# Pair 0's C scaled from PSUM, and four moves in the queues of a fused scan and feed-forward kernel

## The chip, the cores and the metric

The kernel runs on one core of one Trainium2 chip. The metric is the device time of one execution in microseconds (us), the median of several runs. A core has TensorE (PE; its weight loads are PEld), VectorE (DVE), ScalarE (ACT), GpSimd (POOL) and SyncE (SP), each with a queue of its own that is worked off in order. SP, ACT and POOL also issue DMA transfers. PE writes only to PSUM, eight banks of 512 fp32 columns on 128 partitions; the other tiles lie in SBUF.

## What is computed

The first half is a chunked scan over a sequence of 768 for 4 batches and 8 heads, with a state of 16 x 32 per head; its output is fed to a bilinear layer over 3072 tokens (256 to 1536 to 256).

```python
cum = np.cumsum(log_a_chunk, axis=-1)
L = np.exp(cum[..., :, None] - cum[..., None, :]) * causal
M = np.einsum('bhin,bhjn->bhij', Cc, Bc) * L
y = np.einsum('bhij,bhjd->bhid', M, xc) + np.einsum('bhin,bhnd->bhid', Cc, state) * np.exp(cum)[..., None]
state = decay_full * state + sum_j(B_j x_j * decay_from_j)
...
out = ((y @ w_a) * (y @ w_b)) @ w_out
```

## The kernel before, in words

The sequence is cut into 6 blocks of 128 positions, and two batches form a pair, so there are 12 pairs; pair p is block p // 2. Everything is done pair by pair, in an order that is written out by hand for pairs 0 to 2 and by a loop over p = 3 to 11 after that (lines 579 to 778). Each engine gets its instructions in the order of the code.

The decay is split into two factors: fC multiplies C and fB, its reciprocal, multiplies B. Running products of `a` come from `scan` on DVE (L204, one block each), their reciprocal at mid-block from `over_mid` (L207), and `sel_over_mid` (L210, tile selr) spreads it. `factors_mm` (L223) turns them by small fp32 matmuls into a PSUM bank, fps, of 32 columns per block. ACT copies fps to fC; `fb` (L569) makes fB of fC on DVE. For block 0 DVE makes fB straight from fps (L585).

For each pair, `scale_bc` (L261, L253) multiplies B and C by their factors (tiles bm and cm) and `scale_x` (L245, L247) turns x to fp16. For pairs 0 to 3, `transposes` (L288) turns bm and cm on PE; ACT copies the turned B (bt, L299, masked by the constant ch) and DVE the turned C (ct, L300). From pair 4 on, POOL writes bm and cm into the tile planes (L253, L271) and `turn` (L310) has a transposing DMA on SP's queue turn them. `scores` (L322) are 32 small matmuls into the tile SC; `mask` (L356 on DVE, or L353 on ACT with L354 on POOL, through the tile tmp) makes them causal; `pv`, `pv_u` and `outputs` (L365, L399, L427) form the pair's output, and `ds_mm` (L382) the state's increment. ACT copies the output to X2T (L418, L443; for pair 0 L453 and L455; for pair 2 half on ACT, half on DVE, L414 and L415). `state_sums` (L468, L470, tile U) updates the state on DVE and `state_spread` (L486, L493, tiles spair and gU) prepares it on POOL for the pair of the next block; `state` calls both.

The feed-forward layer is cut into 6 units per pair. `unit` has PE make two products of 4 matmuls each, aps (with Wa) and bps (with Wb), at L506; ACT copies aps to asb (L520), and DVE multiplies bps by asb into hk (L527). `out_mm` (L540) multiplies hk by Wo, 12 matmuls for each batch of the pair; ACT copies this down result to osb (L555, `out_store`) and SP stores it (L557). The PSUM tiles aps, bps, ops, fps, py, tb, tc and gps share four banks.

Pair p's B, C and x are loaded in two halves each (`load1`, L126), into one of three buffers. Loads of the start go over the queues of SP, ACT and POOL; POOL also loads the weights (L142, L147). From pair 3 on all loads, all turning transfers and nearly all stores go over SP. The constants ch (from ph, 5 KB) and c32 are loaded at L178 and L165. `warmup` (L197) issues matmuls of zeros whose results nobody reads, so that PE is busy in the start; the text calls them dummies.

Of the kernel before, what the change touches and what calls it, by code (L numbers as in the profile page):

```python
# [9 lines left out]
f32 = mybir.dt.float32  # L10
# [12 lines left out]
def kernel(  # L23
# [13 lines left out]
    nc = tc.nc  # L37
# [4 lines left out]
    NBLK = S // Q  # L42
# [74 lines left out]
    def tiles(p):  # L117
        Bn = inp.tile([128, H, 2, N], f32, name="bn", tag="bn")
        Cn = inp.tile([128, H, 2, N], f32, name="cn", tag="cn")
        Xn = inp.tile([128, H, 2, D], f32, name="xn", tag="xn")  # L120
        pair_in[p] = (Bn, Cn, Xn)

    def load1(eng, p, which, bt, i0=0, n=64):
        blk, bp = divmod(p, NBP)
        src = (B, C, x)[which][2 * bp + bt, :, blk * Q + 2 * i0 : blk * Q + 2 * i0 + 2 * n, :]
        return eng.dma_start(  # L126
            pair_in[p][which][64 * bt + i0 : 64 * bt + i0 + n].rearrange("i h r n -> i h (r n)"),
            src.rearrange("h (i r) n -> i h (r n)", r=2),
        )
# [2 lines left out]
        tiles(p)  # L132
        return [load1(eng or nc.sync, p, w, bt) for w in range(3) for bt in range(2)]

    def load_parts(p):
        tiles(p)
        return lambda w: [load1(nc.sync, p, w, bt) for bt in range(2)]

    def load_w(half):
        c = slice(half * KC, (half + 1) * KC)  # L140
        return [
# [14 lines left out]
    load1(nc.sync, 0, 0, 0)  # L156
    load1(nc.scalar, 0, 1, 1)
    load1(nc.sync, 0, 1, 0, 0, 32)
    load1(nc.scalar, 0, 1, 0, 32, 32)
    nc.scalar.preload_act_table_set("natural_log_exp_and_others")  # L160
    load1(nc.scalar, 0, 2, 1)
    load1(nc.sync, 0, 2, 0)
    load1(nc.scalar, 1, 1, 1)
    load1(nc.sync, 1, 0, 0)
    nc.sync.dma_start(c32, p32_t.ap())  # L165
    nc.vector.memset(warm.bitcast(u32), 0)  # L166
    nc.vector.memset(zero, 0.0)
# [7 lines left out]
        pattern=[[-H, 2], [-2 * H, NBP], [-1, H]],  # L175
        channel_multiplier=1,
    )
    nc.gpsimd.dma_start(ch, ph_t.ap())  # L178
    nc.gpsimd.memset(ident, 1.0)
    nc.gpsimd.affine_select(  # L180
        out=ident, in_=ident, compare_op=ALU.is_equal, fill=0.0, base=0, pattern=[[-1, 128]], channel_multiplier=1
# [20 lines left out]
    def scan(lo, hi):  # L202
        for k in range(lo, hi):
            nc.vector.tensor_tensor_scan(Pr[:, k], a_sb[:, k], zero, 1.0, ALU.mult, ALU.add)  # L204
# [9 lines left out]
            op=ALU.mult,  # L214
        )

    def factors_mm(lo, hi):
        fps = psf.tile([128, 512], f32, name="fps", tag="ff")
        F = fps[:, 0 : (hi - lo) * 2 * NBP * H].rearrange("p (k r c) -> p k r c", k=hi - lo, r=2)
        for k in range(lo, hi):  # L220
            for r in range(2):
                for bt in range(2):
                    nc.tensor.matmul(  # L223
                        F[64 * bt : 64 * bt + 64, k - lo, r],
                        Pr[:, k].rearrange("p (i r) -> p r i", r=2)[:, r],
                        selr[:, k, bt],
                        start=True,
                        stop=True,
                        skip_group_check=True,
                        tile_position=(0, 64 * bt),  # L230
                    )
        return F.rearrange("p k r c -> p (k r c)")

    def flat(f, lo, hi):
        return f[:, lo:hi].rearrange("p k r b h -> p (k r b h)")
# [10 lines left out]
        else:  # L246
            eng.tensor_scalar(xo, xi, XS, None, ALU.mult)  # L247

    def scale_bc(p, which, eng):
        blk, bp = divmod(p, NBP)  # L250
        name, f = (("bm", fB), ("cm", fC))[which]
        if p >= P0 and which:
            eng.tensor_tensor(  # L253
                out=planes[p % 2][:, 4:6].rearrange("p r (h n) -> p r h n", n=N),
                in0=pair_in[p][which].rearrange("p h r n -> p r h n"),
                in1=f[:, blk, :, bp].unsqueeze(3).broadcast_to((128, 2, H, N)),
                op=ALU.mult,
            )
            return
        m_ = mid.tile([128, 2, H, N], f16, name=name, tag=name)  # L260
        eng.tensor_tensor(  # L261
            out=m_,
            in0=pair_in[p][which].rearrange("p h r n -> p r h n"),
            in1=f[:, blk, :, bp].unsqueeze(3).broadcast_to((128, 2, H, N)),
            op=ALU.mult,
        )
        st.setdefault(p, {})[name] = m_
        if p >= P0:
            dst = planes[p % 2][:, 0:4].rearrange("p (r e) (m f n) -> p r e m f n", e=2, f=2, n=N)
            for e in range(2):  # L270
                eng.tensor_copy(dst[:, :, e, :, e], m_.rearrange("p r (m f) n -> p r m f n", f=2)[:, :, :, e])  # L271
# [6 lines left out]
    def transposes(p, ps=None, between=None, apart=False):  # L278
        s = st[p]
        if ps is None:  # L280
            ps = [SC[0], SC[1]] if apart else None
            on_dve = apart
        else:
            on_dve = True
        TB, TC = (TT[:, 0:256], TT[:, 256:512]) if ps is None else [t_.bitcast(f16)[:, 0:256] for t_ in ps]
        for T_, src in ((TB, s["bm"]), (TC, s["cm"])):
            for r in range(2):
                nc.tensor.transpose(  # L288
                    T_[:, r * 128 : (r + 1) * 128], src[:, r].rearrange("p h n -> p (h n)"), ident
                )  # L290
            if between:
                between()
                between = None
        BT = mid.tile([128, 2, 2, 2, 64], f16, name="bt", tag="bt")
        CT = mid.tile([128, 2, Q], f16, name="ct", tag="ct")
        b_ = []
        for e in range(2):
            o_ = BT[:, e].rearrange("p r t i -> p (r t i)")
            b_.append(nc.scalar.activation(out=o_, in_=TB, func=AF.Copy, scale=par[:, e : e + 1]))  # L299
        c_ = (nc.vector.tensor_copy if on_dve else nc.scalar.copy)(  # L300
            CT.rearrange("p t (i r) -> p r (t i)", r=2), TC.rearrange("p (r c) -> p r c", r=2)
        )
        if apart:
            for i_ in b_:
                tc.declare_no_dep(c_.ins, i_.ins.name, reason="reads of two banks")
        s["BT"], s["CT"] = BT, CT
# [276 lines left out]
    sel_over_mid(0, 1, nc.vector)  # L583
    v = factors_mm(0, 1)
    nc.vector.reciprocal(flat(fB, 0, 1), v)  # L585
    nc.scalar.copy(flat(fC, 0, 1), v)
    warmup(2, SC[3])
    warmup(1, SC[3], 128)
    scale_bc(0, 0, nc.vector)
    scale_bc(0, 1, nc.vector)  # L590
    scan(1, 3)
    tb, tcp = bank("tb"), bank("tc")
    transposes(0, [tb, tcp], lambda: warmup(1, SC[3]))
    over_mid(1, 3)
    sel_over_mid(1, 3, nc.vector)
    warmup(1, SC[3])
    warmup(2, SC[3], 128)
    scores(0)
# [2 lines left out]
    mask(product0(0, 1))  # L601
    mask(product0(1, 1), by_pool=True)
    mask(product0(1, 0))
    v = factors_mm(1, 3)
    nc.scalar.copy(flat(fC, 1, 3), v)  # L605
    warmup(2, tcp)
    scale_bc(1, 1, nc.vector)
    scale_bc(1, 0, nc.gpsimd)
    py = [bank("py0"), bank("py1")]
    pv_u(0, 0, py, True)  # L610
# [21 lines left out]
    scale_x(1, nc.scalar)  # L632
    for m in range(2):
        mask(product(1, m))
    over_mid(3, NBLK)
    sel_over_mid(3, NBLK, nc.vector)
    mask(product(1, 2))
    bps = [unit_mm(0, k2, Wb) for k2 in range(3)]
    for bt in range(2):
# [13 lines left out]
    tc.add_manual_dep(x2[0].ins, w1[1].ins.name, AFTER, reason="weights ahead of pair 2's x")  # L653
    for k2 in range(3):
        times(0, k2, bps[k2], asb[k2])
    v = factors_mm(3, NBLK)
    pv(1, DS=(0, SC[:2]))
    ds_mm(0, 64, SC[:2])
    nc.scalar.copy(flat(fC, 3, NBLK), v)
    fb(1)  # L660
    scale_bc(2, 0, nc.gpsimd)
    scale_bc(2, 1, nc.gpsimd)
# [24 lines left out]
    h()  # L687
    scale_x(2, nc.scalar)
    scale(3)
    o = [bank("ops"), bank("ops")]  # L690
    out_mm(0, 0, o[0], range(6))
    out_mm(0, 1, o[1], range(6))
    out_mm(0, 0, o[0], range(6, NK))
    pull(2)
    pv(2, split=True)
    out_mm(0, 1, o[1], range(6, NK))
    h = unit(2, 0)
    transposes(3, apart=True)
    load(4)
    for bt in range(2):  # L700
        out_store(0, bt, o[bt])
    state(2)
    fb(2)
    h()
    h = unit(2, 1)
# [1 line left out]
    for p in range(3, NP):  # L707
        scores(p)
        ri = p >= P0
        if p + 1 < NP:  # L710
            scale(p + 1)
        if p + 2 < NP:
            loads = load_parts(p + 2)
            loads(0)
            if ri:
                loads(1)
        if p + 1 < NP:
            turn(p + 1)
        if p + 2 < NP:
            if not ri:  # L720
                loads(1)
            loads(2)
        if p == 3:
            mask(product(p, 0))
            h()
            for m in range(1, 4):
                mask(product(p, m))
            out_half(1, 0)
            out_half(1, 1)
            go((2, 2))  # L730
        else:
            h = unit(p - 1, 0)
            mask(product(p, 0), ri=ri)
            h()
            mask(product(p, 1), ri=ri)
            mask(product(p, 2), ri=ri)
            h = unit(p - 1, 1)
            h()
            mask(product(p, 3), ri=ri)
            go((p - 1, 2))  # L740
            out_half(p - 2, 0)
            go((p - 1, 3))
        pull(p)
        outputs(p) if ri else pv(p)
        state(p)
        if p == 3:
            go((2, 3))
        else:
            out_half(p - 2, 1)
        if p % 2 == 0 and p // 2 + 1 < NBLK:  # L750
            fb(p // 2 + 1)
        go((p - 1, 4), (p - 1, 5))
# [56 lines left out]
```

## Time and profile before

| what | value |
|---|---|
| median of 3 runs | 128.59 us (128.12 to 130.98) |
| the profiled execution | 130.67 us, its span 129.0 us |
| PE busy | 122.5 us (95%), 1963 matmuls |
| DVE, ACT, POOL busy | 89.0, 72.6, 56.9 us |
| DMA | 13.79 MB in 45877 packets, 40896 of them under 512 B |
| turning transfer (L310) | 8, 2.9 us from issue to landing (median) |
| hk (L527) | 72, 686 ns each |
| asb (L520) | 72, 587 ns each |

The span is the time from the first instruction to the last in the profiled execution; its execution's own time has some 1.7 us around that. A busy PE is not PE at its peak, since the ends of its pipelined matmuls are modelled. In timelines the first column is the start and the second the duration in us, rows that are alike are merged (x8), and brackets hold the idle time ahead of the first and what ended it. ACTq, SPq and POOLq are the queues' own work, mostly the issue of transfers.

### The profile page before, as it was taken

To read this page: it belongs to the slowest core of one execution; us is meant where nothing else is said; L and a number is where in the kernel's file an instruction comes from. 1 tells how busy PE (TensorE), PEld (TensorE's weight loads), DVE (VectorE), ACT (ScalarE), POOL (GpSimd) and SP (SyncE) were. 2 spreads that over 40 slices of the span, in tenths; PEclk is the share of its full clock that TensorE was granted. 3 is DMA by queue.
4 is the path that set the end of the run, shared out by engine and by line. 5 is a ranking of instruction groups with operands and counts; after the bars stand their busy time and mean duration, and the time that the engine had idled before them with its cause. 6 is when DMAs were issued, how large, how long until landed. Compare 5 with 4: busy or idle time off the path is not lost.

```text
span 129.0 us, 4787 instructions
## 1 busy us (share of the span) xinstructions
PE 122.5 (95%) x1963; PEld 102.2 (79%) x1963; DVE 89.0 (69%) x167; ACT 72.6 (56%) x145; POOL 56.9 (44%) x100
## 2 busy tenths in 40 slices
PE   6999979999899998999999999999999999999990
PEld 2454768988588986988988988988898889899980
DVE  1586695985677985884976967967939939834450
ACT  0464646781646547547556576476575485585530
POOL 6979596759662545605607508309128000000000
PEclk9999999999999999999999999999999999999999
DMA  3999999975526569972793473644732210110112
GB/s 67 188 119 232 145 192 175 186 147 86 140 42 119 149 111 116 173 163 74 119 125 92 69 171 80 118 126 88 133 91 76 50 64 5 41 41 5 41 41 81
DMA packets 45877, 13.79 MB, mean 107 GB/s; under 512 B 40896, under 2 KB 45664, under 8 KB 45856
## 3 DMA queue, kind: packets, MB, share of 16 engines
q1 hardware_dynamic: 41376, 10.05, 39.2%
q0 software_dynamic: 1952, 3.02, 14.4%
q10 hardware_dynamic: 2528, 0.43, 2.0%
q8 instruction: 15, 0.25, 0.9%
q14 instruction: 6, 0.05, 0.2%
HBM read 11.13 MB, written 3.15 MB: 111 GB/s over the span
## 4 chain that ended last, share of the span: by engine, by line
PE 77%; DMA 8%; SPq 4%; POOL 3%; ACT 2%; DVE 1%; issue 1%; POOLq 0%; DVEq 0%; ACTq 0%
PE aps L506 22%; PE ops L540 20%; PE bps L506 20%; DMA turned<-planes 4%; SPq L126 3%; PE SC L322 3%; PE SC L365 2%; DMA xn<-in_x_dram 2%; PE tc L197 2%; PE fps L223 2%; DMA a_sb<-in_a_dram 2%; PE SC L197 2%; PE ops L764 1%; PE SC L427 1%; SPq L310 1%
## 5 line engine op out<-in xcount | busy, mean ns | idle before, releaser
L527 DVE TENSOR_TENSOR hk<-bps,asb 128x512 f16<-128x512 f32 x72 | 49.2, 686 | 19.1 <-ACT asb L520 18.2
L520 ACT COPY asb<-aps 128x512 f32<-128x512 f32 x72 | 42.1, 587 | 19.5 <-PE aps L506 18.5
L506 PE MATMUL aps<-X2T,Wa 128*128 128x256 f16 x288 | 44.1, 277 | 0.5 <-ACT X2T L418 0.4
L506 PE MATMUL bps<-X2T,Wb 128*128 128x256 f16 x288 | 42.9, 273 | 0.5 <-ACT osb L555 0.5
L540 PE MATMUL ops<-Wo,hk 128*128 128x256 f16 x276 | 33.9, 273 | 0.0
L506 PEld LDWEIGHTS <-Wa 128*128 128x128 f16 x288 | 29.1, 105 | 4.0 <-issue 0.9
L506 PEld LDWEIGHTS <-Wb 128*128 128x128 f16 x288 | 29.7, 103 | 2.4 <-issue 0.7
L540 PEld LDWEIGHTS <-hk 128*128 128x128 f16 x276 | 26.0, 98 | 3.6 <-DVE hk L527 0.2
L356 DVE TENSOR_TENSOR t<-SC,causal_ri 128x512 f16<-128x512 f32 x32 | 21.1, 680 | 0.1
L555 ACT ACTIVATE osb<-ops 128x256 f32<-128x256 f32 x23 | 8.7, 384 | 15.6 <-PE ops L540 15.4
L486 POOL TENSOR_TENSOR spair<-U,ch 128x128 f16<-128x128 f32 x8 | 3.2, 401 | 31.8 <-DVE U L470 31.8
L247 POOL TENSOR_SCALAR x<-xn 128x512 f16<-128x512 f32 x9 | 13.4, 1492 | 2.3 <-DMA xn<-in_x_dram 1.8
L443 ACT ACTIVATE X2T<-SC 64x256 f16<-64x256 f32 (+1 forms) x24 | 10.9, 456 | 4.8 <-PE SC L382 3.6
L356 DVE TENSOR_TENSOR t<-SC,causal 128x512 f16<-128x512 f32 x13 | 8.3, 682 | 2.5 <-PE SC L322 2.4
L470 DVE SCALAR_TENSOR_TENSOR U<-SC,G,gU 128x64 f32<-128x64 f32 x16 | 4.3, 282 | 6.5 <-ACT X2T L443 5.9
L261 POOL TENSOR_TENSOR bm<-bn,fB 128x256 f16<-128x256 f32 x11 | 7.1, 645 | 0.0
L197 PE MATMUL SC<-warm 128*128 128x512 f16 (+1 forms) x15 | 5.6, 524 | 1.2 <-DVE warm L166 1.2
L253 POOL TENSOR_TENSOR planes<-cn,fC 128x256 f16<-128x256 f32 x8 | 5.0, 622 | 1.9 <-DMA cn<-in_C_dram 1.9
L197 PEld LDWEIGHTS <-warm 128*128 128x128 f16 x21 | 2.4, 133 | 3.9 <-issue 2.6
L354 POOL TENSOR_TENSOR t<-tmp,causal 128x512 f16<-128x512 f32 x3 | 3.5, 1158 | 3.4 <-ACT tmp L353 3.4
L365 PEld LDWEIGHTS <-x 64*32 64x32 f16 x384 | 3.0, 91 | 2.1 <-ACT fC L605 0.8
L365 PE MATMUL SC<-t,x 64*32 64x128 f16 x352 | 4.6, 219 | 0.0
(79 smaller groups left out, 84.5 us busy)
## 6 DMA issues: line engine op xcount, KB each, us to landing
out_dram<-osb SPq DMA_DIRECT2D x23, 128.0 KB, 2.0
xn<-in_x_dram SPq DMA_DIRECT2D x21, 128.0 KB, 3.7
bn<-in_B_dram SPq DMA_DIRECT2D x20, 64.0 KB, 2.9
cn<-in_C_dram SPq DMA_DIRECT2D x18, 64.0 KB, 2.8
Wa<-in_moe_w_a_dram POOLq DMA_DIRECT2D x2, 384.0 KB, 5.5
Wb<-in_moe_w_b_dram POOLq DMA_DIRECT2D x2, 384.0 KB, 6.9
Wo<-in_moe_w_out_dram POOLq DMA_DIRECT2D x2, 384.0 KB, 6.0
xn<-in_x_dram POOLq DMA_DIRECT2D x2, 128.0 KB, 7.1
```

Source lines behind the costliest of these rows:

```text
L197: nc.tensor.matmul(bank[:, 0:cols], warm[:, 0:128], warm[:, 0:cols], start=True, stop=True, skip_group_check=True)
L247: eng.tensor_scalar(xo, xi, XS, None, ALU.mult)
L253: eng.tensor_tensor(out=planes[p % 2][:, 4:6].rearrange("p r (h n) -> p r h n", n=N), in0=pair_in[p][which].rearrange("p h r n -> p r h n" ...
L261: eng.tensor_tensor(out=m_, in0=pair_in[p][which].rearrange("p h r n -> p r h n"), in1=f[:, blk, :, bp].unsqueeze(3).broadcast_to((128, 2, ...
L356: nc.vector.tensor_tensor(out=o_, in0=i_, in1=c_, op=ALU.mult)
L365: nc.tensor.matmul(py[bt, u][32 * (g ^ 2 * bt) : 32 * (g ^ 2 * bt) + 32] if p >= P0 else py[bt][32 * g : 32 * g + 32, u * Q : (u + 1) * Q] ...
L443: nc.scalar.activation(out=X2T[to, p, bt].rearrange("p u (i r) -> p u r i", r=2), in_=SCt[bt][fr, :, 0:Q].rearrange("p u (r i) -> p u r i" ...
L506: nc.tensor.matmul(ps[:, kk * 2 * Q : (kk + 1) * 2 * Q], W[k // 6][:, f, k % 6 // 3 * 384 : (k % 6 // 3 + 1) * 384].rearrange("p (c kk) -> ...
L520: (nc.vector.tensor_copy if on_dve else nc.scalar.copy)(asb, a_ps)
L527: nc.vector.tensor_tensor(out=s["hk"][:, 2 * k2 : 2 * k2 + 2, :].rearrange("p k q -> p (k q)"), in0=b_ps, in1=asb, op=ALU.mult)
L540: nc.tensor.matmul(o_ps[:, 0:d_model], hk[:, k, bt * Q : (bt + 1) * Q], Wo[:, k, :], start=(k == 0), stop=(k == NK - 1), skip_group_check= ...
L555: nc.scalar.activation(out=o_sb, in_=o_ps[:, 0:d_model], func=AF.Copy, scale=1.0 / (YS * YS))
```

## The change

- Pair 0's C is scaled on DVE by the factor as it lies in PSUM (fps), not by its copy fC; ACT makes that copy later, after the transposes' copies.
- The dummy between pair 0's transposes has 128 columns, not 512.
- The loads of ch (from POOL) and of half of pair 1's C (from ACT) go to SP's queue.
- The scans of blocks 1 and 2 stand at two places instead of one; reciprocals and selr of blocks 1 and 2 are made with those of blocks 3 to 5. The factor products of blocks 1 and 2 move from after pair 0's scores to after pair 1's output, into one bank with those of blocks 3 to 5, and one ACT copy takes all five. A third dummy of 512 columns stands where they were.
- Pair 0's two down results are copied and stored right after they are complete, ahead of pair 3's transposes.
- In the loop, the turning transfer of pair p+1 stands ahead of all six loads of pair p+2; before, two or four of those stood ahead of it. On POOL, `state_spread` of pair p-1 moves from the end of its own pass to the next one, between the planes and the scaling of x.

```diff
     load1(nc.sync, 0, 1, 0, 0, 32)
+    nc.sync.dma_start(ch, ph_t.ap())
     load1(nc.scalar, 0, 1, 0, 32, 32)
...
-    load1(nc.scalar, 1, 1, 1)
     load1(nc.sync, 1, 0, 0)
+    load1(nc.sync, 1, 1, 1)
...
-    nc.gpsimd.dma_start(ch, ph_t.ap())
...
-    def factors_mm(lo, hi):
-        fps = psf.tile([128, 512], f32, name="fps", tag="ff")
-        F = fps[:, 0 : (hi - lo) * 2 * NBP * H].rearrange("p (k r c) -> p k r c", k=hi - lo, r=2)
+    def factors_mm(lo, hi, fps=None, k0=0):
+        if fps is None:
+            fps = psf.tile([128, 512], f32, name="fps", tag="ff")
+        w = 2 * NBP * H
+        F = fps[:, k0 * w : (k0 + hi - lo) * w].rearrange("p (k r c) -> p k r c", k=hi - lo, r=2)
...
-    def scale_bc(p, which, eng):
+    def scale_bc(p, which, eng, factor=None):
...
-            in1=f[:, blk, :, bp].unsqueeze(3).broadcast_to((128, 2, H, N)),
+            in1=(f[:, blk, :, bp] if factor is None else factor).unsqueeze(3).broadcast_to((128, 2, H, N)),
...
     nc.vector.reciprocal(flat(fB, 0, 1), v)
-    nc.scalar.copy(flat(fC, 0, 1), v)
...
-    scale_bc(0, 1, nc.vector)
-    scan(1, 3)
+    scale_bc(0, 1, nc.vector, v.rearrange("p (r b h) -> p r b h", r=2, b=NBP)[:, :, 0])
     tb, tcp = bank("tb"), bank("tc")
-    transposes(0, [tb, tcp], lambda: warmup(1, SC[3]))
-    over_mid(1, 3)
-    sel_over_mid(1, 3, nc.vector)
+    transposes(0, [tb, tcp], lambda: warmup(1, SC[3], 128))
+    nc.scalar.copy(flat(fC, 0, 1), v)
+    scan(1, 2)
...
-    v = factors_mm(1, 3)
-    nc.scalar.copy(flat(fC, 1, 3), v)
-    warmup(2, tcp)
+    warmup(3, tcp)
     scale_bc(1, 1, nc.vector)
+    scan(2, 3)
...
-    over_mid(3, NBLK)
-    sel_over_mid(3, NBLK, nc.vector)
+    over_mid(1, NBLK)
+    sel_over_mid(1, NBLK, nc.vector)
...
-    v = factors_mm(3, NBLK)
+    fps = bank("fps")
+    factors_mm(3, NBLK, fps, 2)
     pv(1, DS=(0, SC[:2]))
     ds_mm(0, 64, SC[:2])
-    nc.scalar.copy(flat(fC, 3, NBLK), v)
+    factors_mm(1, 3, fps, 0)
+    nc.scalar.copy(flat(fC, 1, NBLK), fps[:, 0 : (NBLK - 1) * 2 * NBP * H])
...
     scale(3)
+    load(4)
     o = [bank("ops"), bank("ops")]
     out_mm(0, 0, o[0], range(6))
     out_mm(0, 1, o[1], range(6))
     out_mm(0, 0, o[0], range(6, NK))
+    out_store(0, 0, o[0])
     pull(2)
     pv(2, split=True)
     out_mm(0, 1, o[1], range(6, NK))
+    out_store(0, 1, o[1])
     h = unit(2, 0)
     transposes(3, apart=True)
-    load(4)
-    for bt in range(2):
-        out_store(0, bt, o[bt])
-    state(2)
+    state_sums(2)
...
         if p + 1 < NP:
-            scale(p + 1)
+            scale_bc(p + 1, 1, nc.gpsimd)
+            scale_bc(p + 1, 0, nc.gpsimd)
+            turn(p + 1)
+        if (p - 1) // NBP < NBLK - 1:
+            state_spread(p - 1)
+        if p + 1 < NP:
+            scale_x(p + 1, nc.gpsimd)
         if p + 2 < NP:
-            loads = load_parts(p + 2)
-            loads(0)
-            if ri:
-                loads(1)
-        if p + 1 < NP:
-            turn(p + 1)
-        if p + 2 < NP:
-            if not ri:
-                loads(1)
-            loads(2)
+            load(p + 2)
...
-        state(p)
+        if p // NBP < NBLK - 1:
+            state_sums(p)
```

More of the change, by code (lines that the diff above doesn't have):

```diff
@@ L133, in load @@
         return [load1(eng or nc.sync, p, w, bt) for w in range(3) for bt in range(2)]
-    def load_parts(p):
-        tiles(p)
-        return lambda w: [load1(nc.sync, p, w, bt) for bt in range(2)]
     def load_w(half):
```

## Prediction

> **What bounds the kernel now.** I read the page's chain first, then the stage table, then the timeline wherever PE (TensorE) idles. The chain that ended last, by engine:
>
> ```profile
> PE 77%; DMA 8%; SPq 4%; POOL 3%; ACT 2%; DVE 1%; issue 1%; POOLq 0%; DVEq 0%; ACTq 0%
> ```
>
> PE sets the time; the few per cent of others are places where it stood still. The windows view (window; length and busy us of PE, PEld, DVE, ACT, POOL with counts; clock, DMA share, GB/s) says where:
>
> ```profile
> 14.07:18.67 4.60, 3.81 (x137) 3.33 (x137) 4.03 (x8) 2.73 (x6) 3.40 (x5) 1.00 1.07 201
> ...
> 32.38:34.32 1.94, 1.34 (x12) 0.82 (x9) 1.61 (x5) 1.92 (x6) 0.96 (x4) 1.00 0.42 96
> ...
> 60.68:69.82 9.14, 9.14 (x161) 8.00 (x161) 7.18 (x14) 5.66 (x12) 3.94 (x8) 1.00 0.74 110
> 69.82:78.96 9.14, 9.14 (x162) 8.00 (x162) 6.92 (x13) 5.66 (x12) 3.90 (x8) 1.00 0.52 110
> ```
>
> From 60.68 on PE is full: 9.14 us per pair. No edit removes a matmul there, so whatever is to be won lies before 52 us. The timeline of the start (start, duration):
>
> ```profile
> 5.29 0.60 ACTq L126 DMA_DIRECT2D cn<-in_C_dram  x1
> 5.30 0.42 DVE L261 TENSOR_TENSOR bm<-bn,fB 128x256 f16<-128x256 f32 x1
> ...
> 5.94 0.19 ACT L586 COPY fC<-fps 128x32 f32<-128x32 f32 x1 [1.72 <-DVE bm L261]
> ...
> 6.16 0.42 DVE L261 TENSOR_TENSOR cm<-cn,fC 128x256 f16<-128x256 f32 x1 [0.43 <-ACT fC L586]
> ...
> 7.15 0.41 DVE L300 COPY ct<-tc 128x256 f16<-128x256 f16 x1
> ...
> 7.62 0.65 PE L322 MATMUL SC<-ct,bt 32*64 32x128 f16 x32
> ```
>
> ACT issues a transfer (5.29 to 5.89) before it copies fC, so DVE stands idle from 5.72 to 6.16, and transposes, ct and scores follow. The same timeline, later:
>
> ```profile
> 12.19 1.92 PE L506 MATMUL aps<-X2T,Wa 128*128 128x256 f16 x8
> ...
> 14.85 1.47 PE L506 MATMUL bps<-X2T,Wb 128*128 128x256 f16 x12
> ```
>
> Eight matmuls took 1.92 us, then twelve of the same size 1.47: up to about 14 us PE runs at half speed, although the page prints a granted clock of 1.00 there. The two other standstills, from the timeline of 29 to 52 us:
>
> ```profile
> 32.63 0.84 ACT L299 ACTIVATE bt<-SC,ch 128x256 f16<-128x256 f16 x2
> ...
> 33.36 0.66 ACT L555 ACTIVATE osb<-ops 128x256 f32<-128x256 f32 x2
> ...
> 33.80 0.60 PE L506 MATMUL bps<-X2T,Wb 128*128 128x256 f16 x4 [0.54 <-ACT osb L555]
> ...
> 46.80 1.28 SPq L310 DMA_TRANSPOSE turned<-planes  x1
> ...
> 51.55 0.43 PE L322 MATMUL SC<-turned 32*64 32x128 f16 x32 [0.60 <-DMA turned<-planes]
> ```
>
> At 33.80 a product waits for the bank that the first down result is copied out of; that copy stands behind bt on ACT. At 51.55 the scores of pair 5 wait for its turned B and C, whose transfer was issued at 46.80 and took 4.7 us.
>
> **The skill.** "TensorE: Matmul & The Clock Gate", Part 1: PE starts at half clock and is released after a busy window of about 3.4 us that runs freely, so the release varies from run to run. The trace agrees on the halves (0.21 us a matmul early, 0.109 in the full stretch); three runs from 128.12 to 130.98 fit such a variation without showing its cause. "VectorE: DVE Perf Modes", Why PSUM operands drop a tier: a two-tensor fp32 operation runs at one element a cycle from SBUF or PSUM. The trace agrees: 128x512 with a PSUM operand takes 0.69, 128x256 from SBUF 0.42. "DMA: Bandwidth & Descriptors", Issuing engines are not separate DMA queues: moving a transfer to SP saves only issue time. Here such an issue is 0.60 us on ACT and 0.78 on POOL.
>
> **Part 1, the start.** Pair 0's C reads its factor from PSUM. DVE could start at 5.72, but in the trace the last third of C lands at 5.89, so cm starts at about 5.92 instead of 6.16. I price it as before, 0.42; a PSUM operand could add 0.05. The transposes need no wait behind the inserted dummy (128 columns, not 512). ct needs 0.99 from the start of cm (6.16 to 7.15): 6.91 to 7.32, scores at 7.38 instead of 7.62. bt (6.22 to 7.06) is ready. Gain 0.24. DVE's scan of one block (0.36) fits between ct and the masks. fC's copy now comes after bt, and x after it: to about 7.9, while tmp needs ACT at 8.12. PE's sixteen fp32 products and two 512-column dummies (0.76 and 0.96 us in the chain) become three dummies of 0.43, so pair 0's first output waits for its second mask: scores + 0.76 + 1.28 + 0.08 = 9.50, not 9.92. Gain now 0.42, carried to the first up product: 11.77, not 12.19. The weights for it landed at 10.95 and are issued 0.78 earlier, since POOL no longer issues ch.
>
> If the clock release stays at 14.07, that lead is spent at half clock: scores of pair 1 start at 13.62, are 0.45 into a 0.65 us job at the release, and end near 14.18, not 14.40. Lead 0.22. Next is DVE: selr (16.00 to 16.53) held PE's factor products at 16.68. It comes 0.16 earlier with the masks, but has 160 columns, not 96, about 0.07 more. Lead 0.1 to 0.2.
>
> Bounds: POOL's B and C of pair 1 enter the DMA rings 0.78 earlier, against pair 0's C; if that lands 0.4 later, the start loses 0.2 instead. Best is C landing at 5.7: 0.3. The transfer of pair 1's C moves behind B on SP, its issue still near 5.3, needed at 10: hidden. ch on SP must land by 6.2 for bt; its neighbours of that queue land by 5.6, so hidden, else up to 0.3.
>
> **Part 2, factor products 1 and 2 behind pair 1's output.** 16 products; 24 took 0.88 in the chain at 16.70, so 16 take 0.59. They stand where PE waited from about 18.1 to 18.67 for ACT's copy of X2T, so they cost 0 to 0.1; without that cover 0.59. ACT's fC copy (0.23, some 0.06 longer) waits for them and ends near 19.0, ahead of asb at 19.3. fB of block 1 comes some 0.5 later (19.4); POOL uses it at 20.42. Hidden. Start and part 2 together: -0.15.
>
> **Part 3, down results copied sooner.** In the built program the two down results have the banks of pair 2's first and second bps. The first result is complete at 29.7 and ACT is idle until 30.83, so its copy (0.38) is free. The second is complete at 31.4, copied to 31.85 between X2T and asb (32.03). So bt stays at 32.63 to 33.47; the aps at 32.66 moves to 32.43 (its new bank was read by 30.3), bps runs 32.87 to 33.3, and the scores of pair 3 wait for bt: 33.53 instead of 34.32. Gain 0.79, 0.5 if the second copy slips behind asb. The load of pair 4 stays at its place in SP's queue: nothing.
>
> **Part 4, the turning transfer ahead of the loads, POOL's state work behind the planes.** For pair 4: C scaled on POOL from 32.6, B after fB at 33.7, copies to 34.9; turn issued at 35.0 instead of 37.77, landing 2.9 later at 37.9; the scores need it at 40.95. Behind it wait six loads, 0.65 each: 36.3 to 40.2. C of pair 5 then lands near 41.7 (43.0 before), planes take 0.62+0.62+0.53, and its turn is issued at 43.6, landing between 46.5 and 48.3. The scores of pair 5 need it at 50.0 (50.68+0.11-0.79). The wait of 51.55 goes: 0.76. State work moved back on POOL (0.80) is wanted one pair later: hidden by some 8 us. Later pairs are full already: 0.
>
> **Sum.** 0.15 + 0.79 + 0.76 = 1.70 us off the profiled span of 129.0: 127.3 (its execution 130.67 to 129.0). That execution is 2.08 above the median of 128.59; I take the same 1.70 off the median: 126.9.
>
> **Rivals.**
> 1. The turn's wait stays: pair 5's turn is again issued late and lands 4.7 later, because the loads that feed it now queue behind a blocked SP. For it: some issues on SP took 1.5 to 2.2 us. Against: 2 us of slack. Without the 0.76: 127.65.
> 2. The clock is released one window earlier, 10.7: dense matmuls and dummies from 11.8 to 14.0 halve, about 1.3. For it: the gaps near 8 to 10 us shrink. 125.6.
> 3. Released one window later: 4 aps and 12 bps (1.75 us) and the scores double, 1.95, less 0.5 of the DVE wait they cover, and 0.15 of the pv: 1.6. 128.5.
> 4. Slower: SP's loop. Loads of p+2 now wait for the turn of p+1, and that turn for its own loads: turn issue 1.3, B and C 2.6, landing 2.8, planes 1.8 make 8.5 us, under PE's 9.14. If C behind a turn lands 1.8 later (the turn of 46.80 took 4.7, not 2.9), the loop is 10.3; beyond 9.14 each of seven pairs loses 1.2, less 3.0 of slack: +5.4-1.7 = 132.3. Against: stores already pace SP, and the slow landing was one of eight.
>
> **Numbers.** The sum as worked out 0.60 (own range 126.2 to 127.6), rival 1 0.10, rival 2 0.13, rival 3 0.12, rival 4 0.05. The range 125.5 to 128.6 takes in all but rival 4 and the tails. Two per cent, about what a measurement here can tell from no change, is 2.57: under 126.02 come rival 2 and an eighth of the rest, 0.23; over 131.16 rival 4, 0.05; within 0.72.
>
> **What would show it.** Right: cm at about 5.9, scores at 7.4; no standstill near 33.5 or before pair 5's scores; 9.14 us per pair unchanged; turns landing over 2 us before use. Wrong: C landing after 6.2; bt later than 33.5; PE waiting on turned; another release of the clock.

## The result and the profile after

The changed kernel takes 132.71 us (median of 4 runs, 132.47 to 132.94), the kernel before 128.48 (128.12 to 130.98) beside it: 1.031 times as long, 95% interval 1.0242 to 1.0378. The ratios here and below leave out executions over 1.5% above the fastest of their kernel, so they are not quotients of the medians. The changed kernel is slower, and lies outside the range forecast. The profiled execution took 132.94 us, its span 131.2.

The chain that ended last, by engine and, in part, by line:

```profile
PE 85%; DMA 9%; ACT 1%; ACTq 1%; DVE 0%; issue 0%; DVEq 0%
PE aps L504 26%; PE ops L538 24%; PE bps L504 24%; DMA cn<-in_C_dram 9%; PE SC L320 3%; PE SC L363 3%; PE SC L380 1%; PE SC L425 1%; PE fps L221 1%; PE ops L759 1%; ACT bt L297 1%; ACTq L126 1%; PE SC L286 0%; ACT asb L518 0%; PE SC L397 0%
```

The chain's SPq (4%) and POOL (3%) of before are gone, but DMA has 9% now, and all of it is one line: loads of C. The chain cut to the first 24 us names the load (start, length, what):

```profile
1.53 3.11 DMA cn<-in_C_dram
4.64 0.02 issue
4.66 9.24 DMA cn<-in_C_dram
...
13.99 0.44 DVE cm L259
14.43 0.04 issue
14.47 0.39 PE SC L286 x2
```

Half of pair 1's C, issued on SP at 4.66, lands at 13.90. DVE then scales it and PE turns it. The windows of the stretch, with a full pair at the end:

```profile
4.00:10.69 6.69, 5.67 (x93) 2.82 (x91) 3.82 (x8) 2.96 (x9) 5.21 (x8) 1.00 1.12 176
10.69:14.47 3.78, 0.21 (x2) 0.04 (x2) 0.48 (x2) 0.00 (x0) 2.72 (x4) 0.80 1.17 202
14.47:22.54 8.07, 8.06 (x164) 5.85 (x164) 6.15 (x14) 4.11 (x8) 4.03 (x8) 0.67 0.73 142
63.10:72.25 9.15, 9.15 (x176) 8.01 (x177) 7.20 (x14) 5.67 (x12) 3.96 (x8) 1.00 0.70 118
```

In the second window PE works 0.21 of 3.78 us and ACT not at all, while the DMA engines are full (1.17, 202 GB/s): the data flow, but not those that PE waits for. In the third PE is full, yet its granted clock is 0.67 on the mean. The last is the steady pair: 9.15 as before. So the loss is in the start. The timeline of the start and of pair 1 (the first rows answer to those of before):

```profile
4.47 0.76 POOL L138 DMA_DIRECT2D Wa<-in_moe_w_a_dram  x1
4.66 0.60 SPq L126 DMA_DIRECT2D cn<-in_C_dram  x1
...
5.53 0.41 DVE L259 TENSOR_TENSOR cm<-cn,fps 128x256 f16<-128x256 f32 x1
...
6.87 0.44 PE L320 MATMUL SC<-ct,bt 32*64 32x128 f16 x32 [0.21 <-DVE ct L298]
```
```profile
14.47 0.39 PE L286 MATMUL SC<-ident,cm 128*128 128x128 f16 x2 [3.57 <-DVE cm L259]
...
15.09 1.91 PE L504 MATMUL aps<-X2T,Wa 128*128 128x256 f16 x8
...
18.34 2.19 PE L504 MATMUL bps<-X2T,Wb 128*128 128x256 f16 x12
```

Pair 0 is quicker than forecast: cm at 5.53 and scores at 6.87, at full clock (0.44 for 32 matmuls, 0.65 before). Then PE waits, 3.57 us by the bracket at 14.47, and afterwards twelve bps take 2.19 us, where before they took 1.47. The clock events in the trace say why: full clock from 6.16, half from 12.99 to 19.81, full after that. The two later places, from the timeline of 33 to 55 us:

```profile
33.70 0.39 ACT L553 ACTIVATE osb<-ops 128x256 f32<-128x256 f32 x1 [0.86 <-PE ops L538]
...
35.29 0.38 ACT L553 ACTIVATE osb<-ops 128x256 f32<-128x256 f32 x1 [0.34 <-PE ops L538]
...
36.63 0.60 PE L504 MATMUL bps<-X2T,Wb 128*128 128x256 f16 x4
```
```profile
53.84 0.43 PE L320 MATMUL SC<-turned 32*64 32x128 f16 x32
```

Both standstills are gone: the down results are copied out ahead of bt, bps has no bracket, and the scores of pair 5 wait for nothing.

Where the time goes is read from a few marks on PE (start in us), here with two further profiles from the experiments below:

| mark | before, as predicted from | before, second profile | after | after, ch back on POOL |
|---|---|---|---|---|
| first up product | 12.19 | 11.79 | 15.09 | 10.97 |
| scores of pair 1 | 14.04 | 12.76 | 16.93 | 11.94 |
| first up product behind pair 1's output | 18.67 | 17.39 | 22.54 | 16.90 |
| scores of pair 2 | 27.29 | 26.01 | 31.17 | 25.56 |
| scores of pair 3 | 34.32 | 33.04 | 37.28 | 31.92 |
| scores of pair 5 | 51.55 | 49.60 | 53.84 | 48.91 |
| span | 129.0 | 127.0 | 131.2 | 126.3 |

Against the second profile of before, after is 3.30 us late at the first up product, 5.15 behind pair 1's output, 4.24 at the scores of pair 3, and 4.2 at the end.

### The profile page after: what moved, and what is told of

It reads as the page before. It is cut to its first block, busy times and chain, and to the rows that moved or that the text cites. A ratio compares the mean times of both kernels' runs of the same rounds, so it can differ in the third digit from the quotient of the medians.

```text
span 131.2 us, 4785 instructions
## 1 busy us (share of the span) xinstructions
PE 122.2 (93%) x1964; PEld 102.5 (78%) x1964; DVE 88.6 (68%) x165; ACT 72.6 (55%) x144; POOL 55.7 (42%) x99
## 4 chain that ended last, share of the span: by engine, by line
PE 85%; DMA 9%; ACT 1%; ACTq 1%; DVE 0%; issue 0%; DVEq 0%
PE aps L504 26%; PE ops L538 24%; PE bps L504 24%; DMA cn<-in_C_dram 9%; PE SC L320 3%; PE SC L363 3%; PE SC L380 1%; PE SC L425 1%; PE fps L221 1%; PE ops L759 1%; ACT bt L297 1%; ACTq L126 1%; PE SC L286 0%; ACT asb L518 0%; PE SC L397 0%; DVE cm L259 0%
## 5 line engine op out<-in xcount | busy, mean ns | idle before, releaser
L504 PE MATMUL aps<-X2T,Wa 128*128 128x256 f16 x288 | 44.6, 279 | 0.0
L504 PE MATMUL bps<-X2T,Wb 128*128 128x256 f16 x288 | 43.6, 276 | 0.0
L193 PE MATMUL SC<-warm 128*128 128x512 f16 (+1 forms) x15 | 4.9, 473 | 1.2 <-DVE warm L163 1.2
L297 ACT ACTIVATE bt<-SC,ch 128x256 f16<-128x256 f16 x6 | 2.5, 471 | 4.3 <-PE SC L286 4.2
```

The costliest lines, as they stand in the source:

```text
L193: nc.tensor.matmul(bank[:, 0:cols], warm[:, 0:128], warm[:, 0:cols], start=True, stop=True, skip_group_check=True)
L504: nc.tensor.matmul(ps[:, kk * 2 * Q : (kk + 1) * 2 * Q], W[k // 6][:, f, k % 6 // 3 * 384 : (k % 6 // 3 + 1) * 384].rearrange("p (c kk) -> ...
```

## The experiments

**Which of the two moved transfers?** Theory A: SP's queue makes C late. Theory B: the weights do, which POOL issues at 4.47 instead of 5.53 since it no longer issues ch, and which overtake C in the DMA engines. First, C back on ACT (ch stays on SP):

```diff
+    load1(nc.scalar, 1, 1, 1)
     load1(nc.sync, 1, 0, 0)
-    load1(nc.sync, 1, 1, 1)
```

> The changed kernel with one load moved back: half of pair 1's C goes over ACT's queue again, ch stays on SP. Theory A (the load is late because it stands on SP's queue behind x and B and is then overtaken by the weight stream; in the changed kernel it landed at about 13.9 us): on ACT it lands near 8.5 us, PE's standstill of 3.7 us at 10.7 us goes, and so does the second half-clock stretch (12.98 to 19.81 us); time 126 to 128 us. Theory B (the load is late because POOL, without ch, issues the weights about 1.06 us earlier, whichever queue the load is on): C still lands after 12 us, time 131 to 133 us.

Measured: 132.25 us, ratio to before 1.0301 (1.0251 to 1.0352). C was issued on ACT at 4.70 and landed at 13.58, and PE stood until 14.15:

```profile
14.15 0.39 PE L286 MATMUL SC<-ident,cm 128*128 128x128 f16 x2 [3.25 <-DVE cm L259]
```

Theory A falls. Second, ch back on POOL (C stays on SP):

```diff
-    nc.sync.dma_start(ch, ph_t.ap())
...
+    nc.gpsimd.dma_start(ch, ph_t.ap())
     nc.gpsimd.memset(ident, 1.0)
```

> The changed kernel with the other transfer moved back: ch is loaded by POOL again, so that POOL's weight loads are issued about 1 us later; half of pair 1's C stays on SP. Theory A (SP's queue): C still lands late, near 13 us, time 131 to 133 us. Theory B (weights issued earlier): C lands before 10 us, time 126 to 128 us. If both are needed for the delay, this run and the one with C on ACT are both fast.

Measured: 127.65 us, 0.9929 (0.9905 to 0.9953). Of all kernels here it is the one whose gain is surest. C was issued at 4.33, Wa at 5.51, and PE has no such wait. Third, both edits:

> The changed kernel with both transfers on the queues that they had before; every other part stays. Both theories of the transfers: C lands near 8.4 us, no standstill at 10.7 us, time near 126.5 us, since the standstills at 33 us and 51 us stay away (1.55 us) and the start gains a little. A third theory, that the start is slow for another reason (the moved factor products or the read of PSUM), gives over 130 us.

Measured: 127.61 us, 0.9946 (0.9912 to 0.9979). That is 1.1 us above what I expected; part of what held it back comes with the last experiment. But with ch back on POOL it makes no difference in which of the two queues C is, and moving ch costs 5 us.

**Is ch alone enough, without the quicker start?** The kernel before, with ch moved and nothing else:

```diff
     load1(nc.sync, 0, 1, 0, 0, 32)
+    nc.sync.dma_start(ch, ph_t.ap())
...
-    nc.gpsimd.dma_start(ch, ph_t.ap())
```

> The kernel before with one line moved: ch (5 KB) is loaded by SP instead of POOL; half of pair 1's C stays on ACT. Theory B (POOL's weights, issued some 0.8 us earlier, overtake pair 1's C in the DMA engines): C lands after 12 us instead of 8.4, PE stands still some 3 us before the transpose of cm(1), the time is 131 to 133. Rival D (it takes the change's quicker start as well: only a C that is needed earlier is late): C lands before 10 and the time is that of before, 128 to 128.8. Theory A (queue of SP) has already failed.

Measured: 133.65 us, 1.0369 (1.0266 to 1.0473), a little over theory B's range. Its chain of the first 24 us:

```profile
4.87 10.30 DMA cn<-in_C_dram
```

The one line makes the whole loss; C lands at 15.16. The rest of the change isn't needed for it.

**Is it the time at which the weights start?** The changed kernel with four short memsets on POOL ahead of the weights:

```diff
+    for _ in range(4):
+        nc.gpsimd.memset(planes[0][:, 0:4].bitcast(u32), 0)
     load_w(0)
```

> The changed kernel, both transfers still on SP, with four memsets on POOL (0.2 to 0.3 us each, about 1.1 in all) ahead of the first weight load, on a tile that is zeroed anyway; so the weights are issued when they were in the kernel before. Theory B: pair 1's C lands before 10 us, no standstill of 3.7 us, 127 to 128 as with ch back on POOL (127.65). Rival E (it is ch on SP, and not the time at which the weights start, that makes C late): C still lands after 12 and the time stays near 132.5.

Measured: 128.15 us, 0.9972 (0.9937 to 1.0006). The weights were issued at 5.91, C landed at 8.58. Both transfers are on SP here, as in the changed kernel, and holding the weights back by 1.4 us gains 4.6 us. The median is a little over the range that theory B gave. The clock has to do with that: in eight of the twenty executions its mean was under 0.99 and their median is 129.14, in the other twelve it is 127.88. The profiled execution is one of the eight (windows; the last three figures are clock, DMA share and GB/s):

```profile
7.52:10.93 3.41, 2.01 (x40) 0.81 (x39) 3.21 (x5) 1.82 (x5) 3.35 (x5) 1.00 1.02 136
10.93:14.34 3.41, 3.41 (x47) 2.04 (x46) 1.85 (x7) 1.65 (x4) 2.65 (x4) 0.50 1.09 198
```

PE had no wait over 0.42 us in the first of the two, and the clock was halved in the second all the same. No run here shows what took it.

**Does it matter which queue C is in, and is it C?** The half of C issued by POOL ahead of the weights:

```diff
-    load1(nc.sync, 1, 1, 1)
...
     load1(nc.gpsimd, 1, 1, 0)
+    load1(nc.gpsimd, 1, 1, 1)
     load_w(0)
```

> The changed kernel with the second half of pair 1's C issued by POOL, behind its first half and ahead of the weights, in the queue of the weights instead of beside it. Theory B (a load in another queue gets only one small packet for each large packet of the weights; one queue is worked off in order): C lands before 9 us, no standstill, the clock is released near 6 and kept, 126.5 to 127.7. If the load of C is slow in itself when issued this late, it lands after 12 and the time is above 131.

Measured: 128.70 us, 0.9963 (0.9927 to 0.9999). C lands at 8.80 as expected and no long wait is left, but the time is a miss, a microsecond above what I expected: the weights come 0.7 later than in the changed kernel, PE waits for them (0.42 and 0.17 us), and in ten of its twenty executions the mean clock was under 0.99. This run moves two things, C's queue and the weights' start. To part them, two halves were swapped between the queues and the weights left at 4.47:

```diff
     load1(nc.sync, 1, 0, 0)
-    load1(nc.sync, 1, 1, 1)
+    load1(nc.sync, 1, 0, 1)
...
-    load1(nc.gpsimd, 1, 0, 1)
+    load1(nc.gpsimd, 1, 1, 1)
```

> The changed kernel with two halves swapped between queues: the half of pair 1's C that SP issued is issued by POOL at 2.9 us, in the place of a half of pair 1's B, and that half of B is issued by SP in C's place near 4.7. The weights stay at 4.47. Theory B (whichever load is issued behind the weights in another queue crawls): C lands before 9, B after 12; PE stands still some 3 us, now before the transpose of bm(1), and the time stays at 131 to 133. Rival H (POOL's queue is what helped in the run with C on POOL, so a C in it is enough; or it is C itself that is slow): no standstill of that length, 127 to 128.5.

Measured: 133.42 us, 1.0354 (1.0259 to 1.045), a little over the range. Now C lands early and B crawls; the chain and PE's timeline:

```profile
4.77 8.97 DMA bn<-in_B_dram
```
```profile
14.58 0.39 PE L286 MATMUL SC<-ident,bm 128*128 128x128 f16 x2 [3.75 <-POOL bm L259]
```

It is not C, and a C in POOL's queue is no cure: each half that was issued behind the weights and outside their queue, C on SP or ACT and B on SP, was late. Ten profiles side by side, in the order of the lead (issue of Wa less issue of the last half of pair 1's C, of B in the last row but one):

| kernel | last half issued | Wa issued | lead | landed |
|---|---|---|---|---|
| after, weights later | 4.73 | 5.91 | 1.18 | 8.58 |
| after, C on POOL | 4.48 | 5.15 | 0.67 | 8.80 |
| before, turn only | 5.06 | 5.45 | 0.39 | 8.51 |
| before, as predicted from | 5.29 | 5.53 | 0.24 | 8.36 |
| before, down results only | 5.38 | 5.49 | 0.11 | 11.09 |
| before, second profile | 5.34 | 5.35 | 0.01 | 10.88 |
| after | 4.66 | 4.47 | -0.19 | 13.90 |
| after, C on ACT | 4.70 | 4.47 | -0.23 | 13.58 |
| after, halves swapped (B) | 4.77 | 4.47 | -0.30 | 13.75 |
| before, ch only | 4.87 | 4.47 | -0.40 | 15.16 |

The four other profiles fit in: leads of 1.18 (ch on POOL), 0.60 (both back), 0.29 (start only) and -0.12 us (the dummies below), with the last mark of C's landing at 8.40, 8.25, 9.52 and 13.21. The kernel before stood at the edge: its lead is 0.0 to 0.2 us, and C lands just in time or a little late. The packets in the trace show it too. C's half is 512 packets of 128 bytes, the weights come in packets of 1536. With ch on POOL, 389 and 415 small packets are moved in two half microseconds (5.5 to 6.5), before the weights begin near 7. In the changed kernel, from 10 to 12 us, each half microsecond moves 18 to 41 small packets, one to three for each of the 16 engines, beside some four large ones for each. The Trainium skill, "DMA: Bandwidth & Descriptors", SWDGE vs HWDGE vs iDMA, says that each DMA engine takes turns between its inner queues and that POOL's transfers and those of SP and ACT feed different ones. That agrees with those counts, and with the table. How the turns are shared out stays open. One small packet for each large one, as theory B had it when C went to POOL, is not what the counts show: from 10 to 12 us they are 123 small to 246 large (1536 or 4096 bytes).

**How much of the loss is the clock?** The changed kernel, with 17 dummies of 512 columns between the two transposes of pair 1, so that PE is busy while C is late:

```diff
-    transposes(1, apart=True)
+    transposes(1, apart=True, between=lambda: warmup(17, tcp))
```

> The changed kernel with 17 more dummy matmuls of 512 columns between the transposes of pair 1's B and those of its C, where PE stands still for 3.7 us; they do no work that is used. If the standstill alone were the loss, the time stays at 132.7 us. If the standstill also takes the clock away (half clock from 12.98 to 19.81 us), the dummies keep it, and the matmuls of that stretch from 14.5 us on run at full clock: about 2.2 us less, near 130.5 us.

Measured: 130.98 us, 1.0215 (1.0163 to 1.0268). The stretch with the dummies, the one behind it, and the first transpose of C:

```profile
10.69:14.15 3.46, 3.46 (x19) 1.57 (x18) 0.85 (x3) 0.00 (x0) 2.67 (x4) 1.00 1.17 215
14.15:20.45 6.30, 5.88 (x165) 4.87 (x163) 5.64 (x13) 4.00 (x8) 3.57 (x5) 1.00 0.68 129
```
```profile
14.36 0.28 PE L286 MATMUL SC<-ident,cm 128*128 128x128 f16 x2
```

C's transposes start at 14.36 us, about as late as in the changed kernel (14.47), though it is the last dummies that hold them here: DVE scaled C from 13.30 on, in the changed kernel from 13.99. But the clock stays at 1.00, and from these transposes to the first up product behind pair 1's output (20.45) PE takes 6.09 instead of 8.07 us. All four executions had a mean clock of 0.997 or more, those of the changed kernel 0.974. So of the 5.06 us between the kernel with ch back on POOL (127.65) and the changed kernel, about 1.7 are the clock that the standstill took away (2.2 were expected), and about 3.3 the standstill.

**What are the other parts worth, and from what time?** The prediction had one profile of before, of 130.67 us. Another one:

> The kernel before, unchanged, for another profile of it. The prediction took its steps from an execution of 130.67 us whose clock was released at 14.07 us. If that release explains the 2.1 us to the median, an execution near 128.4 shows a release near 6 to 11 us, and twelve bps of pair 0's first unit take about 1.3 us from start to end; the waits near 33.5 and 51.5 us are in it too. If the release is at 14 again, the difference between executions is elsewhere.

Measured: 128.71 us (1.0004, 0.9969 to 1.004); the profiled execution took 128.73, its span is 127.0, and its clock was released at 4.45 us instead of 14.07. From its timelines:

```profile
13.57 1.47 PE L506 MATMUL bps<-X2T,Wb 128*128 128x256 f16 x12
```
```profile
32.51 0.60 PE L506 MATMUL bps<-X2T,Wb 128*128 128x256 f16 x4 [0.54 <-ACT osb L555]
```
```profile
49.60 0.43 PE L322 MATMUL SC<-turned 32*64 32x128 f16 x32
```

The wait for the bank is here again, the wait for turned tiles (0.60 at 51.55 before) is not: its transfer was issued at 44.87 and landed after 2.8 us, not at 46.80 and after 4.7. The bps took 1.47, not the 1.3 that I expected of a full clock. At the scores of pair 5 this execution is 1.95 us ahead of the first one: 1.28 of it stand already at the scores of pair 1, up to which the first ran at half clock, and 0.67 come between the scores of pairs 3 and 5, where the first waited for turned tiles. So about two thirds of it go with the clock, although C landed 2.5 us later here. Then each part alone on the kernel before; the loop's part:

```diff
-            scale(p + 1)
...
+            scale_bc(p + 1, 1, nc.gpsimd)
+            scale_bc(p + 1, 0, nc.gpsimd)
             turn(p + 1)
+        if (p - 1) // NBP < NBLK - 1:
+            state_spread(p - 1)
...
+            load(p + 2)
...
```

> The kernel before with the loop's part alone: the turning transfer ahead of all six loads, the state's spreading behind the planes on POOL. The prediction's sum gives 0.76 us for it, that is 127.9 against about 128.6. Rival F: the slow transfer of 4.7 us was an accident of one execution (the second profile of the kernel before has no wait for turned tiles), so against the median the part is worth 0 to 0.2 us.

Measured: 128.36 against 128.74 us, 0.9974 (0.9954 to 0.9993): 0.33 us (0.09 to 0.59) by the ratio, less than the 0.76 of the sum, and not clearly apart from rival F. The down results (the load of pair 4 goes ahead with them, so that it keeps its place in SP's queue):

```diff
+    load(4)
...
     out_mm(0, 0, o[0], range(6, NK))
+    out_store(0, 0, o[0])
...
     out_mm(0, 1, o[1], range(6, NK))
+    out_store(0, 1, o[1])
...
-    load(4)
-    for bt in range(2):
-        out_store(0, bt, o[bt])
```

> The kernel before with the down results' part alone: pair 0's two down results copied right after they are complete. The prediction's sum gives 0.79 us, and the wait for the bank (0.70 at 33.80 before) is in both profiles of the kernel before: 127.8 to 128.0 against about 128.6. Rival: bt or asb becomes the wait in its place, and nothing is won.

Measured: 128.28 against 128.74 us, 0.9974 (0.9949 to 0.9999): 0.33 us (0.01 to 0.66), less than expected. The wait itself is gone; scores of pair 2 to scores of pair 3 take 6.11 us in its profile and 7.03 in both of before. Why no more of these 0.92 us shows in the time stays open. And the start, both transfers left alone (its main lines):

```diff
-    scale_bc(0, 1, nc.vector)
-    scan(1, 3)
+    scale_bc(0, 1, nc.vector, v.rearrange("p (r b h) -> p r b h", r=2, b=NBP)[:, :, 0])
...
+    factors_mm(1, 3, fps, 0)
...
```

> The kernel before with the start's part alone, both transfers left where they were: C from PSUM, shorter dummy, factor products of blocks 1 and 2 behind pair 1's output. The prediction's sum gives 0.15 us. Rival G: the weights' landing near 11 us bounds the first up product, so that the 0.4 us won ahead of it end in a wait for Wa, and the part is worth nothing, within 0.2 us either way.

Measured: 128.80 against 128.74 us, 1.0011 (0.9986 to 1.0036), that is from 0.18 us faster to 0.46 slower. No gain is seen, as rival G said, but the sum's 0.15 lies in the interval too. The wait that rival G named is there, in this kernel and, longer, in the one with both transfers back (third experiment):

```profile
11.12 1.05 PE L508 MATMUL aps<-X2T,Wa 128*128 128x256 f16 x8 [0.15 <-DMA Wa<-in_moe_w_a_dram]
```
```profile
11.73 1.06 PE L504 MATMUL aps<-X2T,Wa 128*128 128x256 f16 x8 [0.82 <-DMA Wa<-in_moe_w_a_dram]
```

Wa lands at 11.08 and 11.69; before that no first up product can start, however early pair 0 is done. In the first of the two the wait takes just 0.15 us, and behind pair 1's output (16.88) its PE is 0.51 ahead of the second profile of before; so the wait alone doesn't tell why the medians show no gain. By the ratios the three parts add up to about 0.5 us, and the kernel that has all three without the transfers gained 0.69 (0.27 to 1.13): no contradiction.

## Why the prediction was wrong

**The step that failed** is in Part 1: "The transfer of pair 1's C moves behind B on SP, its issue still near 5.3, needed at 10: hidden." The transfer was issued earlier than that, at 4.66, and landed at 13.90. That term was put at nothing and cost 5.1 us: some 3.3 of waiting and 1.7 of clock. I priced a moved load by its place in its own queue. What set its landing was another queue: the sentence ahead, "The weights for it landed at 10.95 and are issued 0.78 earlier", counted the weights' earlier start as help alone, though B and C of pair 1 were the next loads that share the engines with them. The bound that I named, POOL's loads against pair 0's C, looked at the wrong victim: pair 0's cm started at 5.53, 0.39 earlier than forecast. Both issue times of the margin stood in the profile of before: 5.29 for C, 5.53 for Wa. A step that takes 0.78 from POOL's queue turns a lead of 0.24 into a lag. C's own move was not needed for it: left on ACT, with ch alone moved, it landed at 15.16. I had read from the shared engines that a move saves only issue time; that they are shared is just why the order of issue across queues counts.

**The clock.** My rivals 2 and 3 had the release come by chance a window earlier or later. It was released at 6.16, early; no rival had it taken away again. The Trainium skill, "TensorE: Matmul & The Clock Gate", HAM oscillation, says that a gap in PE's work of more than about 3.4 us drops the clock back. The traces agree in part. With a gap of 3.57 us the clock was at half for 6.83 us from 12.99 on, and dummies in the gap kept it. But 3.25 us (C on ACT) was enough too, and in the profiles of the weights later and of the down results only the clock fell for 3.41 us with no wait of PE over 0.45 us in the 3.4 us ahead. So a long gap is not the only way to lose it; what the other way is, no run here shows. That page was at hand, but I had no gap of that length in my working.

**Rival 4, the slower one,** named SP's loop; 9.15 us per pair and no wait on turned tiles show it did not happen. That its time, 132.3, is near the one measured is a coincidence.

**Part 2** was nearly right: the 16 factor products took 0.66 us (0.59 forecast); from the scores of pair 1 to the first up product behind its output the start-only kernel takes 4.77 us, the one with ch back on POOL 4.96, both profiles of before 4.63, so they cost 0.1 to 0.3, not 0 to 0.1.

**The start** was cautious in its times up to pair 0's output. What they are worth stays open: 0.15 was forecast, and the run can't tell that from nothing. That the weights' landing comes next was in the working (10.95, taken to be earlier than needed), and it took 0.15 and 0.82 us.

**Part 3** has the mechanism and, in the traces, the size: 0.92 us less from scores to scores with this part alone (0.79 forecast). In the time it is 0.33, with an interval from 0.01 to 0.66, which leaves the 0.79 out.

**Part 4** has the mechanism, too large: 0.76 was the wait of one execution. The other profile of before has no such wait, and the part alone gained 0.33. With the part in, a slow transfer can still be late: with ch back on POOL the turn of pair 5 was issued at 44.37, landed at 48.87, and PE waited 0.36.

**The sum.** Without the moved ch the change brought 0.91 us (0.60 to 1.22), not 1.70. I took 1.70 off the median, though 0.76 of it was a wait that the execution 2.08 above the median had and another one had not; one profile of a kernel whose runs differ by 2 us can't price a wait that only some have.

## What to carry to other kernels

A load's landing depends on what else enters the DMA engines just ahead of it, so when an issue is taken out of one queue, list what that queue then issues earlier and which small loads of other queues it meets. Compare issue times across queues: a lead of 0.2 us of a small load over a big one is a margin to be kept, if need be by holding the big load back. Price a late load twice, by the wait and by what a clock lost in that wait makes of the work behind it; and don't price a wait from one execution if the runs scatter by more than the wait.

## What the runs showed of the hardware

- A load of 512 packets of 128 bytes landed 3.1 to 4.4 us after its issue if that was 0.24 us or more ahead of the issue of the weights on POOL (packets of 1536 bytes), 5.5 to 5.7 us after it with a lead of 0.0 to 0.1, and 8.6 to 10.3 us after it if issued 0.1 to 0.4 us behind. Queues of SP and ACT did equally badly (13.90 and 13.58).
- With a standstill of PE of 3.57 us the clock was halved for 6.83 us (also with 3.75 us in the run with swapped halves and 4.44 with ch only), with one of 3.25 us (C on ACT) for 3.41 us. Dummies in the gap kept it. In two profiles it was halved for 3.41 us without a standstill.
- Scaling C with its factor in PSUM took 0.41 us in the changed kernel and 0.42 with ch back on POOL, with the factor in SBUF 0.43 and 0.41 there: no price for the PSUM operand in this shape.
